# Sums of exponentials over partitions: TensorE's matmuls of a constant in place of GpSimd's reduction

## The chip, the cores and the metric

One Trainium2 chip, one of its cores. The metric is the device time of one execution in microseconds; lower is better.

## The reference

Causal attention with a memory term, then two feed-forward blocks, all in fp32:

```
scores = q @ k^T / sqrt(D), masked above the diagonal       (B, H, S, D = 4, 8, 576, 64)
a      = exp(scores - max);  a /= sum(a) + 1e-9
local  = a @ v
q_p    = phi(q)                                             phi(x) = max(x, exp(x) - 1) + 1 in effect
mem    = (q_p @ M_prev) / (q_p . z_prev + 1e-6)
attn   = g * mem + (1 - g) * local                          g = sigmoid(beta), per head
x      = attn as (2304, 512)
x      = ((x @ w1) * (x @ w2)) @ w3 @ w_out                 d_ff = 1024
h      = x @ w_in;  out = (h * tanh(softplus(h))) @ w_out2  d_ff = 2048
```

What matters here is sum(a): for every head and query, the sum of the exponentials over all keys.

## The kernel before

Heads are worked on in pairs t = 0, 1. A task is a pair of one batch; the four pairs of batch 0 are split into halves of 288 queries, so there are 8 half tasks and 12 whole ones. A task's queries are cut into ranges (one of 288, two of 144, or three of 192), 48 in all, and each range is one step.

Scores lie transposed: keys on the 128 partitions, queries along the free axis, one block for each tile of keys. So the maximum and the sum over keys run over partitions. A step is recorded as these functions:

- SC: score matmuls into a pair of banks ("gp" in the profile), masks, the elementwise maximum over the blocks on VectorE into m ("t"), and then the maximum over partitions on GpSimd (line 556).
- SE: scores minus maximum on VectorE (line 386, "e<-gp,t"), which frees the gp banks, and the exponential on ScalarE. The exponentials E ("e") have four buffers.
- AV, recorded in the step after: E times V. Each pair of heads has 64 output rows per head, done as four matmuls of 32 columns that write the four quarters of one bank ("g<-e,V"), then a copy to mnl on ScalarE.
- SUM, called by AV: adds of E's blocks on VectorE into S (and a copy on ScalarE where the second block is shorter), then partition_all_reduce with add on GpSimd (line 597, "S<-S").
- At a task's last range AV sends the memory term's norm R and row 0 of S through DRAM (d0) into a column layout cp, takes reciprocals there, sends them back broadcast ("Rr"), multiplies mnl by them, adds both terms and splits the result into "x", the input of the feed-forward block. mnl has two buffers.
- MEM: the memory term's matmuls. The first group of a task also holds four matmuls of 32 columns for R, in the same bank behind the outputs.

Between the steps stand fill units: the loading, conversion and products of the first block's weights (fill_w3, fill_w12; "w3" is multiplied with w_out beforehand), and 96 units of the first feed-forward block (ffn1, ffn1o), each 24 matmuls of 288 columns. The main loop gives out units by a credit that grows in each step by RATE, is capped at CMAX, and leaves RES of the ready units untouched. After the last step the remaining units run among the loads of the second block.

Nothing is issued in recorded order. Every operation goes to a recorder with an engine, an estimated cost, its reads and its writes. schedule() then runs a list schedule in estimated time and issues in that order; each engine, and SyncE's one DMA queue, works strictly in that order on the chip. TensorE takes the ready operation recorded first (fill units with a bias GB); other engines take the one with the longest chain behind it, where every operation that feeds TensorE has TensorE's whole remaining chain behind it. An operation of TensorE counts as ready only PEM ns after data from another engine are there. PSUM has four "g" banks and two pairs of "gp" banks.

Of the kernel before, what the change touches and what calls it, by code (L numbers as in the profile page):

```python
# [15 lines left out]
P = 128  # L16
# [4 lines left out]
    AB=10000,  # L21
    GB=200,
    SPLIT=(0,),
    W3P=3,
    W12P=(3, 10),
    RATE=(1.675, 0.949, 2.526, 4.511, 3.527),
    RES=1,
    WARM=40,
    CMAX=3,
    SPM=100,  # L30
    DMM=800,
    PEM=500,
    LA=2,
    F2N=0,
    MIX=10,
# [258 lines left out]
def kernel(  # L294
# [43 lines left out]

    BUFS = {
# [3 lines left out]
        "f": 5, "s": 4, "q": 8, "b": 8, "r": 4, "G": 2, **CFG.get("BUFS", {}),  # L343
    }
# [6 lines left out]
    def buf(tag, shape, dtype=F32):  # L351
        pool = wp if tag[0] == "w" else ROOMS.get(tag, A1)
        return Buf(pool, shape, dtype, tag, BUFS[tag])
# [3 lines left out]
    def gbuf():  # L357
        return Buf(psG, [P, 512], F32, "g", 4)
# [5 lines left out]
    def dma(dst, src, nbytes, r=(), w=()):  # L364
        op("sp", max(500, nbytes / 340.0), lambda: nc.sync.dma_start(out=dst(), in_=src()), r, w)  # L365

    def mm(o, lhsT, rhs, start, stop):
        nc.tensor.matmul(out=o, lhsT=lhsT, rhs=rhs, start=start, stop=stop)  # L368
# [88 lines left out]
    class Task:  # L457


        def __init__(self, g, hfs):  # L460
            self.g, self.hfs = g, hfs
            self.b, self.p = divmod(g, NP)
            self.w = HS * len(hfs)
            self.x0 = HS * hfs[0]
            self.nj = NJ if 1 in hfs else 3
            self.ranges = RANGES[hfs]
            self.e = {}

        def qs(self, q0, q1):
            return slice(q0 - self.x0, q1 - self.x0)  # L470
# [25 lines left out]

    def MEM(T):
        T.mnl = buf("mnl", [P, 2, T.w])
        T.S = buf("S", [P, 2 * T.w])
        T.R = buf("R", [P, T.w // 4])  # L500
        PH, mnl, R, M = T.PH, T.mnl, T.R, T.M
        n = T.w // 4
        for y, hf in enumerate(T.hfs):
            ps = gbuf()
            qs = T.qs(HS * hf, HS * hf + HS)

            def f(ps=ps, qs=qs, y=y):
                for g in range(4):
                    mm(ps.tile[32 * g:32 * g + 32, 0:HS], M.tile[:, 2 + 32 * g:34 + 32 * g], PH.tile[:, qs], True, True)
                if y == 0:  # L510
                    for g in range(4):
                        mm(ps.tile[32 * g:32 * g + 32, HS:HS + n], M.tile[:, 0:32], PH.tile[:, n * g:n * g + n], True, True)

            op("pe", 1.667 * (HS + (n if y == 0 else 0)) + 100, f, r=[PH, M], w=[ps])
            if y == 0:
                act(n, lambda: R.tile, lambda ps=ps: ps.tile[:, HS:HS + n], [ps], [R], True)
            act(HS, lambda qs=qs: mnl.tile[:, 0, qs], lambda ps=ps: ps.tile[:, 0:HS], [ps], [(mnl, (0, hf))], True)

    def SC(T, r):
        qa, qb, tiles = T.ranges[r]  # L520
        n = qb - qa
        d = T.ld
        m = T.m = buf("t", [P, 2 * n])
        T.s = []
        pair = lambda: m.tile.rearrange("p (t n) -> p t n", t=2)
        for i, pieces in enumerate(tiles):
            s = Buf(psA, [P, 2, 512], F32, "gp", 2)
            T.s.append(s)

            def f(s=s, pieces=pieces):  # L530
                for j, q0, q1, c in pieces:
                    kc = (j * P + K3) % SK
                    for t in range(2):
                        mm(s.tile[:, t, c:c + q1 - q0], d.tile[HALF[t], kc:kc + P], d.tile[HALF[t], SK + q0:SK + q1], True, True)

            op("pe", sum(2 * max(0.833 * (q1 - q0), 107) + 10 for _, q0, q1, _ in pieces) + (300 if i == 0 else 0), f, r=T.reads, w=[s])
            part = lambda x, s=s: s.tile[:, :, x[3]:x[3] + x[2] - x[1]]
            mine = lambda x: pair()[:, :, x[1] - qa:x[2] - qa]

            def masks(todo, s=s):  # L540
                for j, q0, q1, c in todo:
                    a, b = max(q0, j * P), min(q1, j * P + P)
                    if a < b:
                        o = lambda c=c + a - q0, w=b - a: s.tile[:, :, c:c + w]
                        op("dve", t_dve(2 * (b - a)), lambda o=o, j=j, a=a, b=b: nc.vector.tensor_tensor(  # L545
                            out=o(), in0=o(), in1=mask[:, a - j * P:b - j * P].unsqueeze(1).to_broadcast([P, 2, b - a]), op=ALU.add), r=[s, fm_], w=[s])

            rest = pieces
            if i == 0:
                masks(pieces[:1])  # L550
                act(2 * n, pair, lambda x=pieces[0], part=part: part(x), [s], [m], True)
                rest = pieces[1:]
            masks(rest)
            for x in rest:
                tt(2 * (x[2] - x[1]), lambda x=x: mine(x), lambda x=x, part=part: part(x), lambda x=x: mine(x), ALU.max, [s, m], [m])
        op("pool", 430 + 2.85 * 2 * n, lambda: nc.gpsimd.partition_all_reduce(m.tile, m.tile, P, bass_isa.ReduceOp.max), r=[m], w=[m])  # L556
# [23 lines left out]
    def SUM(T, r):  # L580

        qa, qb, tiles = T.ranges[r]
        n = qb - qa
        S_, z = T.S, (T.S, r)
        flat = lambda: S_.tile[:, 2 * (qa - T.x0):2 * (qb - T.x0)]
        sv = lambda q0, q1: flat().rearrange("p (t n) -> p t n", t=2)[:, :, q0 - qa:q1 - qa]
        ev = lambda x, q0=None: x[0].tile[:, :, x[1][3] + (q0 - x[1][1] if q0 else 0):x[1][3] + x[1][2] - x[1][1]]
        todo = [(E, x) for E, pieces in T.e[r] for x in pieces]
        first, second = todo[:2]
        q0 = second[1][1]  # L590
        if q0 > qa:
            act(2 * (q0 - qa), lambda: sv(qa, q0), lambda: ev(first)[:, :, 0:q0 - qa], [first[0]], [z])
        tt(2 * (qb - q0), lambda: sv(q0, qb), lambda: ev(first, q0), lambda: ev(second), ALU.add, [first[0], second[0], z], [z])
        for x in todo[2:]:
            a, b = x[1][1:3]
            tt(2 * (b - a), lambda a=a, b=b: sv(a, b), lambda x=x: ev(x), lambda a=a, b=b: sv(a, b), ALU.add, [x[0], z], [z])
        op("pool", 430 + 5.5 * 2 * n, lambda: nc.gpsimd.partition_all_reduce(flat(), flat(), P, bass_isa.ReduceOp.add), r=[z], w=[z])  # L597

    def AV(T, r):
        qa, qb, tiles = T.ranges[r]  # L600
        n = qb - qa
        mnl, W, p = T.mnl, T.w, T.p
        ps = gbuf()
        for x, (E, pieces) in enumerate(T.e[r]):

            def f(E=E, pieces=pieces, x=x):
                for y, (j, q0, q1, c) in enumerate(pieces):
                    for t in range(2):
                        for h in range(2):
                            a = 64 * t + 32 * h  # L610
                            mm(ps.tile[a:a + 32, q0 - qa:q1 - qa], Vf.tile[:, T.i % 2, j, t, 32 * h:32 * h + 32], E.tile[:, t, c:c + q1 - q0],
                               x == y == 0, x == len(tiles) - 1 and y == len(pieces) - 1)

            op("pe", sum(2 * max(0.833 * (q1 - q0), 55) + 30 for _, q0, q1, _ in pieces) + (300 if x == 0 else 0), f, r=[E, (Vf, T.i % 2)], w=[ps])
        act(n, lambda: mnl.tile[:, 1, T.qs(qa, qb)], lambda: ps.tile[:, 0:n], [ps], [(mnl, (1, r))], True)
        SUM(T, r)
        if r < len(T.ranges) - 1:
            return
        ce = W // 32
        R, S_ = T.R, T.S  # L620
        d0 = Buf(dram, [4, W], F32, f"d0_{W}", 2)
        d1 = Buf(dram, [P, ce], F32, f"d1_{W}", 2)
        cp = buf("cp", [P, ce])
        rb = buf("Rr", [P, 2, W])
        for t in range(2):
            dma(lambda t=t: d0.tile[t].rearrange("(g e) -> g e", g=4), lambda t=t: R.tile[t:97 + t:32], 9216, r=[R], w=[(d0, 2 + t)])
        for x, (qa, qb, _) in enumerate(T.ranges):
            dma(lambda a=qa - T.x0, b=qb - T.x0: d0.tile[2:4, a:b].rearrange("(o t) w -> o t w", o=1),
                lambda a=qa - T.x0, b=qb - T.x0: S_.tile[0:1, 2 * a:2 * b].rearrange("o (t w) -> o t w", t=2), 9216, r=[(S_, x)], w=[(d0, (1, x))])
        dma(lambda: cp.tile, lambda: d0.tile.rearrange("r (c e) -> (r c) e", e=ce), 9216, r=[(d0, 2), (d0, 3)] + [(d0, (1, x)) for x in range(len(T.ranges))], w=[cp])  # L630
        cv = lambda: cp.tile
        ts = lambda s, o: lambda: nc.vector.tensor_scalar(out=cv(), in0=cv(), scalar1=s, scalar2=None, op0=o)
        op("dve", 140, ts(eps, ALU.add), r=[cp], w=[cp])
# [420 lines left out]
    for i in range(NS_ + 1):  # L1054
# [33 lines left out]
        def fills(lst):  # L1088
            rec.bias = CFG["GB"]
            for f in lst:  # L1090
                f()
            rec.bias = 0

        fills(mine[0:third])
        SE(T, r)
        fills(mine[third:2 * third])
        if r == 0:
            if T.i + 2 < len(tasks):
# [120 lines left out]
```

## Time and profile before

| | |
|---|---|
| median of 3 runs | 918.91 us (917.59 to 920.21) |
| profiled execution | 921.47 us, its span 919.60 us |
| TensorE busy | 891.5 us (97%) |
| VectorE busy | 735.0 us (80%) |
| ScalarE busy | 445.8 us (48%) |
| GpSimd busy | 196.7 us (21%) |

In the profile's rows PE is TensorE, PEld its weight loads, DVE VectorE, ACT ScalarE, POOL GpSimd, SP SyncE, which issues the transfers. "out<-in" names what is written and read. What stands in brackets is the idle time of the engine just before, and whose work ended it. The last score step lies near 445 us; from then on only the feed-forward blocks run.

### The profile page before, as it was taken

To read this page: it belongs to the slowest core of one execution; us is meant where nothing else is said; L and a number is where in the kernel's file an instruction comes from. 1 tells how busy PE (TensorE), PEld (TensorE's weight loads), DVE (VectorE), ACT (ScalarE), POOL (GpSimd) and SP (SyncE) were. 2 spreads that over 40 slices of the span, in tenths; PEclk is the share of its full clock that TensorE was granted. 3 is DMA by queue.
4 is the path that set the end of the run, shared out by engine and by line. 5 is a ranking of instruction groups with operands and counts; after the bars stand their busy time and mean duration, and the time that the engine had idled before them with its cause. 6 is when DMAs were issued, how large, how long until landed. Compare 5 with 4: busy or idle time off the path is not lost.

```text
span 919.6 us, 20164 instructions
## 1 busy us (share of the span) xinstructions
PE 891.5 (97%) x7992; PEld 809.9 (88%) x7992; DVE 735.0 (80%) x1490; ACT 445.8 (48%) x806; POOL 196.7 (21%) x102
## 2 busy tenths in 40 slices
PE   8899999999999999999999999999999999999998
PEld 6444788777889898898999999999999999999997
DVE  7988999799887678766647598975759999888884
ACT  5569945454444444534335476343426554334431
POOL 3421145655554433444200000000000000000000
PEclk9999999999999999999999999999999999999999
DMA  7668723222323222210169957633325344433441
GB/s 277 219 192 301 252 69 95 92 79 73 96 75 72 72 69 71 59 43 28 27 203 364 370 185 235 214 138 135 130 107 181 144 142 154 137 127 128 131 131 61
DMA packets 60806, 130.49 MB, mean 142 GB/s; under 512 B 11884, under 2 KB 22308, under 8 KB 60712
## 3 DMA queue, kind: packets, MB, share of 16 engines
q1 hardware_dynamic: 60712, 129.20, 42.6%
q8 instruction: 63, 1.03, 0.5%
q14 instruction: 31, 0.25, 0.1%
HBM read 94.80 MB, written 34.37 MB: 140 GB/s over the span
## 4 chain that ended last, share of the span: by engine, by line
PE 59%; DVE 2%; DMA 1%; POOL 0%; issue 0%; ACT 0%; SPq 0%; DVEq 0%; POOLq 0%; ACTq 0%
PE g L368 40%; PE k L368 17%; PE gp L368 1%; DMA Rr<-d 1%; DVE e L386 0%; POOL t L556 0%; DVE S L386 0%; SPq L365 0%; DVE t L386 0%; DVE G L983 0%; DVE mnl L386 0%; DVE u L371 0%; ACT e L378 0%; POOL S L597 0%; DVE gp L545 0%
## 5 line engine op out<-in xcount | busy, mean ns | idle before, releaser
L597 POOL PARTITION_ALL_REDUCE S<-S x48 | 124.1, 2587 | 151.1 <-DVE S L386 106.8
L376 ACT CAST b<-r 128x896 fp32r<-128x896 f32 (+1 forms) x100 | 83.7, 850 | 113.6 <-PE k L368 42.3
L371 DVE TENSOR_TENSOR b<-r,b 128x896 fp32r<-128x896 f32 (+1 forms) x100 | 96.3, 976 | 21.5 <-ACT b L376 21.0
L368 PE MATMUL g<-x,wB 128*128 128x288 f32 x768 | 112.3, 300 | 0.8 <-ACT mnl L376 0.8
L368 PEld LDWEIGHTS g<-x,wB 128*128 128x128 f32 x768 | 104.7, 190 | 5.6 <-issue 2.4
L368 PE MATMUL g<-u,wA 128*128 128x288 f32 x768 | 109.0, 298 | 0.1
L368 PEld LDWEIGHTS g<-u,wA 128*128 128x128 f32 x768 | 103.2, 188 | 5.3 <-issue 2.6
L556 POOL PARTITION_ALL_REDUCE t<-t x48 | 74.2, 1548 | 105.9 <-DVE t L386 94.6
L386 DVE TENSOR_TENSOR e<-gp,t 128x768 f32<-128x768 f32 (+8 forms) x116 | 66.5, 607 | 21.6 <-POOL t L556 21.4
L386 DVE TENSOR_TENSOR r<-r 128x128 f32<-128x128 f32 (+2 forms) x232 | 77.2, 356 | 2.0
L368 PEld LDWEIGHTS gp<-ld 64*128 64x128 f32 x672 | 52.6, 191 | 22.8 <-issue 9.6
L368 PE MATMUL gp<-ld 64*128 64x192 f32 (+6 forms) x672 | 63.3, 321 | 9.3 <-DVE e L386 6.5
L378 ACT ACTIVATE e<-e 128x512 f32<-128x512 f32 (+4 forms) x64 | 54.8, 870 | 29.5 <-DVE e L386 29.2
L368 PE MATMUL g<-wB,wD 128*128 128x512 f32 x128 | 61.6, 625 | 5.8 <-DVE wD L666 3.5
L368 PE MATMUL g<-x,wD 128*128 128x288 f32 x384 | 57.5, 299 | 2.3 <-ACT mnl L376 2.2
L368 PE MATMUL g<-e,V 128*32 128x192 f32 (+6 forms) x1344 | 54.3, 301 | 3.2 <-ACT mnl L376 2.5
L368 PEld LDWEIGHTS g<-x,wD 128*128 128x128 f32 x384 | 52.7, 189 | 5.0 <-ACT mnl L376 2.9
L368 PE MATMUL g<-x,wE 128*128 128x288 f32 x384 | 55.4, 300 | 1.2 <-ACT mnl L376 1.2
L368 PEld LDWEIGHTS g<-x,wE 128*128 128x128 f32 x384 | 51.8, 188 | 4.0 <-ACT mnl L376 1.5
L386 DVE TENSOR_TENSOR t<-gp,t 128x384 f32<-128x384 f32 (+5 forms) x120 | 52.3, 437 | 1.7
L376 ACT CAST u<-t 128x288 fp32r<-128x288 f32 x64 | 27.4, 429 | 53.2 <-DVE t L386 52.9
L368 PEld LDWEIGHTS g<-e,V 128*32 128x32 f32 x1344 | 36.9, 111 | 18.3 <-issue 4.0
(145 smaller groups left out, 1773.5 us busy)
## 6 DMA issues: line engine op xcount, KB each, us to landing
r<-gd SPq DMA_DIRECT2D x72, 256.0 KB
gd<-G SPq DMA_DIRECT2D x32, 512.0 KB
u<-in_moe_w_dram SPq DMA_DIRECT2D x26, 512.0 KB
s<-in_moe_w_out_dram SPq DMA_DIRECT2D x16, 512.0 KB
s<-in_moe_w_in_dram SPq DMA_DIRECT2D x16, 512.0 KB
ld<-in_qk_dram SPq DMA_DIRECT2D x12, 608.0 KB
Rr<-d SPq DMA_DIRECT2D x24, 288.0 KB
kept<-f SPq DMA_DIRECT2D x11, 512.0 KB
```

The lines of the kernel that those rows point to most:

```text
L368: nc.tensor.matmul(out=o, lhsT=lhsT, rhs=rhs, start=start, stop=stop)
L371: eng.tensor_tensor(out=o, in0=a, in1=b, op=ALU.subtract)
L376: op("act", t_act(n, psum), lambda: nc.scalar.copy(out=o(), in_=i()), r, w)
L378: op("act", t_act(n, psum) + more, lambda: nc.scalar.activation(out=o(), in_=i(), func=func, **kw), r, w)
L386: op(eng, t_dve(n) if eng == "dve" else t_pool(n), lambda: e.tensor_tensor(out=o(), in0=a(), in1=b(), op=alu), r, w)
L556: op("pool", 430 + 2.85 * 2 * n, lambda: nc.gpsimd.partition_all_reduce(m.tile, m.tile, P, bass_isa.ReduceOp.max), r=[m], w=[m])
L597: op("pool", 430 + 5.5 * 2 * n, lambda: nc.gpsimd.partition_all_reduce(flat(), flat(), P, bass_isa.ReduceOp.add), r=[z], w=[z])
```

## The change

The reduction on GpSimd is dropped. SUM's adds stay, but SUM is recorded right behind SE, and S has one buffer per range. Behind a range's last AV matmuls stand four matmuls of a constant 128 x 32 of ones, each over a quarter of S, which write the columns n to n + n/2 of the outputs' bank; the last AV operation now reads S too. ScalarE copies these columns into N, ahead of the outputs. A task's sums go from N to DRAM in two transfers, one per head, in place of one per range. Constants of the planner and of the fill are others: fill weights come a step later (W3P, W12P), the rates are mostly lower, RES and CMAX higher, the margin PEM is 700 in place of 500, and the estimated costs of score and AV operations are a little lower.

```diff
-    W3P=3,
-    W12P=(3, 10),
-    RATE=(1.675, 0.949, 2.526, 4.511, 3.527),
-    RES=1,
+    W3P=2,
+    W12P=(4, 10),
+    RATE=(1.575, 1.069, 2.544, 3.632, 3.318),
+    RES=2,
     WARM=40,
-    CMAX=3,
+    CMAX=5,
...
-    PEM=500,
+    PEM=700,
...
     def MEM(T):
-        T.S = buf("S", [P, 2 * T.w])
+        T.N = buf("N", [P, T.w // 2])
...
     def SUM(T, r):
-        S_, z = T.S, (T.S, r)
-        flat = lambda: S_.tile[:, 2 * (qa - T.x0):2 * (qb - T.x0)]
-        sv = lambda q0, q1: flat().rearrange("p (t n) -> p t n", t=2)[:, :, q0 - qa:q1 - qa]
+        z = T.z[r] = buf("S", [P, 2 * n])
+        sv = lambda q0, q1: z.tile.rearrange("p (t n) -> p t n", t=2)[:, :, q0 - qa:q1 - qa]
...
-        op("pool", 430 + 5.5 * 2 * n, lambda: nc.gpsimd.partition_all_reduce(flat(), flat(), P, bass_isa.ReduceOp.add), r=[z], w=[z])
...
     def AV(T, r):
+                if x == len(tiles) - 1:
+                    for g in range(4):
+                        mm(ps.tile[32 * g:32 * g + 32, n:n + n // 2], one.to_broadcast([P, 32]), z.tile[:, n // 2 * g:n // 2 * g + n // 2], True, True)
...
-            op("pe", sum(2 * max(0.833 * (q1 - q0), 55) + 30 for _, q0, q1, _ in pieces) + (300 if x == 0 else 0), f, r=[E, (Vf, T.i % 2)], w=[ps])
+            more = [z] if x == len(tiles) - 1 else []
+            op("pe", sum(2 * max(0.833 * (q1 - q0), 55) + 12 for _, q0, q1, _ in pieces) + (150 if x == 0 else 0) + (0.833 * n + 12 if more else 0), f,
+               r=[E, (Vf, T.i % 2)] + more, w=[ps])
+        c = (qa - T.x0) // 2
+        act(n // 2, lambda c=c: T.N.tile[:, c:c + n // 2], lambda: ps.tile[:, n:n + n // 2], [ps], [(T.N, r)], True)
         act(n, lambda: mnl.tile[:, 1, T.qs(qa, qb)], lambda: ps.tile[:, 0:n], [ps], [(mnl, (1, r))], True)
-        SUM(T, r)
...
-        for x, (qa, qb, _) in enumerate(T.ranges):
-            dma(lambda a=qa - T.x0, b=qb - T.x0: d0.tile[2:4, a:b].rearrange("(o t) w -> o t w", o=1),
-                lambda a=qa - T.x0, b=qb - T.x0: S_.tile[0:1, 2 * a:2 * b].rearrange("o (t w) -> o t w", t=2), 9216, r=[(S_, x)], w=[(d0, (1, x))])
+            dma(lambda t=t: d0.tile[2 + t].rearrange("(r h e) -> h r e", r=k, h=2), lambda t=t: N.tile[64 * t:64 * t + 33:32].rearrange("h (r e) -> h r e", r=k), 9216,
+                r=[(N, x) for x in range(k)], w=[(d0, 4 + t)])
...
         SE(T, r)
+        SUM(T, r)
```

## Rows read from the trace of the kernel before

**Rows 1.** Busy time by engine in four stages; then clock, DMA share, GB/s.
```profile
0.00:100.00 100.00, 89.10 (x524) 50.09 (x525) 84.44 (x177) 70.07 (x130) 28.68 (x17) 0.97 0.76 258
100.00:280.00 180.00, 168.67 (x1956) 145.16 (x1955) 160.26 (x349) 95.84 (x210) 94.83 (x49) 0.97 0.32 92
280.00:452.00 172.00, 170.63 (x1717) 151.76 (x1715) 125.84 (x259) 74.89 (x167) 70.82 (x37) 1.00 0.21 56
452.00:919.60 467.60, 463.12 (x3802) 462.91 (x3800) 364.48 (x706) 205.00 (x301) 2.40 (x1) 1.00 0.49 168
```
**Rows 2.** Timeline of TensorE, the idle times: start, duration, what, idle before and its releaser.
```profile
21.57 1.12 PE L368 MATMUL g<-wB,wD 128*128 128x512 f32 x2 [2.05 <-DVE wB L666]
...
28.68 1.13 PE L368 MATMUL g<-wB,wD 128*128 128x512 f32 x2 [2.64 <-DVE wD L666]
...
48.67 1.02 PE L368 MATMUL g<-e,V 128*32 128x288 f32 x24 [1.47 <-ACT mnl L376]
...
125.17 0.76 PE L368 MATMUL gp<-ld 64*128 64x144 f32 x8 [1.83 <-DVE e L386]
...
195.63 1.85 PE L368 MATMUL g<-x,wB 128*128 128x288 f32 x12 [0.81 <-ACT mnl L376]
...
220.56 2.31 PE L368 MATMUL g<-x,wD 128*128 128x288 f32 x12 [2.18 <-ACT mnl L376]
...
242.19 2.06 PE L368 MATMUL g<-e,V 128*32 128x192 f32 x56 [0.98 <-ACT mnl L376]
...
259.51 3.44 PE L368 MATMUL g<-x,wE 128*128 128x288 f32 x24 [1.24 <-ACT mnl L376]
```
**Rows 3.** Busy times and granted clock in one stretch behind an idle time, columns as above.
```profile
125.70:129.20 3.50, 3.50 (x24) 3.04 (x26) 3.16 (x9) 1.07 (x3) 0.68 (x1) 0.57 0.72 224
```
**Rows 4.** Timelines of GpSimd (the first) and VectorE around the idle times.
```profile
25.56 3.59 POOL L597 PARTITION_ALL_REDUCE S<-S  x1 [3.52 <-DVE S L386]
...
25.71 2.92 DVE L666 SCALAR_TENSOR_TENSOR wD<-wD,u 128x512 int32<-128x512 int32 x1
...
44.44 0.68 DVE L666 SCALAR_TENSOR_TENSOR wD<-wD,u 128x512 int32<-128x512 int32 x1
...
19.38 2.13 DVE L666 SCALAR_TENSOR_TENSOR wB<-wB,wA 128x512 int32<-128x512 int32 x1
...
214.16 2.32 DVE L386 TENSOR_TENSOR mnl<-mnl,Rr 128x1152 f32<-128x1152 f32 x1 [0.25 <-DMA Rr<-d]
...
236.33 1.35 DVE L386 TENSOR_TENSOR mnl<-mnl,Rr 128x1152 f32<-128x1152 f32 x1
...
192.87 2.02 DVE L386 TENSOR_TENSOR mnl<-mnl 128x576 f32<-128x576 f32 x1
...
257.69 0.75 DVE L386 TENSOR_TENSOR mnl<-mnl 128x576 f32<-128x576 f32 x1
...
118.14 1.22 DVE L386 TENSOR_TENSOR S<-e,S 128x288 f32<-128x288 f32 x1
```
**Rows 5.** Groups of instructions: count, then busy us, mean ns, idle before.
```profile
L597 POOL PARTITION_ALL_REDUCE S<-S x48 | 124.1, 2587 | 151.1 <-DVE S L386 106.8 <-issue 28.0 <-ACT S L376 13.8
```
**Rows 6.** Timeline of TensorE, MEM's two groups and what follows each.
```profile
401.28 0.94 PE L368 MATMUL g<-PH,M 128*32 128x288 f32 x16
402.15 1.85 PE L368 MATMUL g<-x,wB 128*128 128x288 f32 x12
403.93 0.69 PE L368 MATMUL g<-PH,M 128*32 128x288 f32 x8
404.55 1.85 PE L368 MATMUL g<-x,wD 128*128 128x288 f32 x12
```
**Rows 7.** Groups of instructions up to 480 us, shapes apart: R's copy.
```profile
L376 ACT COPY R<-g 128x144 f32<-128x144 f32 x12 | 3.4, 282 | 4.4 <-PE g L368 4.4
```
**Rows 8.** Timeline of all engines around one AV: its matmuls and the last add.
```profile
388.71 1.62 PE L368 MATMUL g<-e,V 128*32 128x192 f32 x40
...
390.99 0.55 DVE L386 TENSOR_TENSOR S<-e,S 128x384 f32<-128x384 f32 x1
```

More of the change, by code (lines that the diff above doesn't have):

```diff
@@ L466, in __init__ @@
             self.ranges = RANGES[hfs]
-            self.e = {}
+            self.e, self.z = {}, {}
         def qs(self, q0, q1):
@@ L534, in f @@
                         mm(s.tile[:, t, c:c + q1 - q0], d.tile[HALF[t], kc:kc + P], d.tile[HALF[t], SK + q0:SK + q1], True, True)
-            op("pe", sum(2 * max(0.833 * (q1 - q0), 107) + 10 for _, q0, q1, _ in pieces) + (300 if i == 0 else 0), f, r=T.reads, w=[s])
+            op("pe", sum(2 * max(0.833 * (q1 - q0), 107) + 10 for _, q0, q1, _ in pieces) + (200 if i == 0 else 0), f, r=T.reads, w=[s])
             part = lambda x, s=s: s.tile[:, :, x[3]:x[3] + x[2] - x[1]]
@@ L602, in AV @@
         mnl, W, p = T.mnl, T.w, T.p
-        ps = gbuf()
+        ps, z = gbuf(), T.z[r]
         for x, (E, pieces) in enumerate(T.e[r]):
@@ L619, in AV @@
         ce = W // 32
-        R, S_ = T.R, T.S
+        R, N, k = T.R, T.N, len(T.ranges)
         d0 = Buf(dram, [4, W], F32, f"d0_{W}", 2)
@@ L626, in AV @@
             dma(lambda t=t: d0.tile[t].rearrange("(g e) -> g e", g=4), lambda t=t: R.tile[t:97 + t:32], 9216, r=[R], w=[(d0, 2 + t)])
-        for x, (qa, qb, _) in enumerate(T.ranges):
-            dma(lambda a=qa - T.x0, b=qb - T.x0: d0.tile[2:4, a:b].rearrange("(o t) w -> o t w", o=1),
-                lambda a=qa - T.x0, b=qb - T.x0: S_.tile[0:1, 2 * a:2 * b].rearrange("o (t w) -> o t w", t=2), 9216, r=[(S_, x)], w=[(d0, (1, x))])
-        dma(lambda: cp.tile, lambda: d0.tile.rearrange("r (c e) -> (r c) e", e=ce), 9216, r=[(d0, 2), (d0, 3)] + [(d0, (1, x)) for x in range(len(T.ranges))], w=[cp])
+            dma(lambda t=t: d0.tile[2 + t].rearrange("(r h e) -> h r e", r=k, h=2), lambda t=t: N.tile[64 * t:64 * t + 33:32].rearrange("h (r e) -> h r e", r=k), 9216,
+                r=[(N, x) for x in range(k)], w=[(d0, 4 + t)])
+        dma(lambda: cp.tile, lambda: d0.tile.rearrange("r (c e) -> (r c) e", e=ce), 9216, r=[(d0, x) for x in range(2, 6)], w=[cp])
         cv = lambda: cp.tile
```

2 rows, old and new, of the table BUFS are left out of this document.

## The prediction

> **What bounds the kernel now.** I read the busy times by stage first, then TensorE's timeline for its idle times, then the timelines of VectorE and GpSimd in front of each of them. By stage [rows 1], TensorE is busy for 463 of the last 468 us: after 452 us it is the bound and nothing there is touched. The diff acts on the first 452 us. There TensorE stands idle 10.9 us up to 100, 11.3 us from 100 to 280, and only 1.4 us from 280 to 452. So a microsecond of matmuls added after 280 us costs a microsecond; before, it may fall into a hole. VectorE is the fullest engine beside it, 160 of 180 us in the second stage.
>
> The idle times are few and long [rows 2]: each row gives in brackets how long TensorE stood and whose result ended it. They end on VectorE's wB, wD and e, or on ScalarE's copies to mnl, which themselves wait for a buffer that VectorE's x work frees. Right behind five idle times of 1.79 to 2.64 us lies a stretch of some 3.4 us in which the granted clock is at the lower level, 1.2 in place of 2.4 GHz; one of the five stands in [rows 3] (the window is a little wider, so its mean is 0.57). TensorE is busy in it, so each costs about 3.4/2 = 1.7 us, together 8.5. With the 23.6 us of idle time, 32 us is all that smoother feeding can give.
>
> Why VectorE is late is seen beside GpSimd [rows 4]. At 25.56 GpSimd begins a sum over partitions (3.59 us); VectorE's operation on wD begins at 25.71 and lasts 2.92 us, while the same operation takes 0.68 us at 44.44. It ends at 28.63, and TensorE's idle time ends at 28.68. So too the operation on wB at 19.38 (2.13), the first product on mnl at 214.16 (2.32 against 1.35 at 236.33), the sum on mnl at 192.87 (2.02 against 0.75 at 257.69), an add into S at 118.14 (1.22, against some 0.45 for a tensor operation of that size). VectorE operations that read two tensors in SBUF are held while GpSimd reduces. Those that read PSUM keep their duration.
>
> **What is removed.** The 48 sums on GpSimd, 124.1 us of that engine [rows 5], and with them their holds. I go through the idle times and take what a normal duration would have left:
> - 21.57 and 28.68: 2.13 - 0.68 = 1.45 and 2.92 - 0.68 = 2.24, and the low clock behind the second, 1.7: together 5.4 us.
> - 48.67 (1.47 us, a copy to mnl that waits behind VectorE): sums also lie in front of it, but no hold ends right at it. I count 1.0.
> - 125.17: 1.22 - 0.45 = 0.8 of the 1.83, some 0.3 from small held operations on cp, and the low clock, 1.7: 2.8 us.
> - 195.63: the sum on mnl was held 1.27, the idle time was 0.81, and VectorE's arrears show once more at the next idle time; I count 1.4.
> - 220.56: 2.32 - 1.35 = 1.0 of the 2.18, and the low clock, 1.7: 2.7 us.
> - 242.19: a held sum on mnl again; all 0.98.
> - 259.51: here VectorE waited for the reciprocals' round trip through DRAM. It starts 2.5 us sooner without the GpSimd sum, which is more than the 1.24 us: 1.2.
>
> Together 15.5 us. Two more idle times of the 1.8 to 2.2 us kind, which end at 94 and 173 us, I leave: there ScalarE was full, or the maximum on GpSimd held VectorE, and that stays. Bounds: nothing if other late work stands behind each held operation, 32 us if everything goes.
>
> **What is added on TensorE.** Per range of n queries four matmuls of 32 columns of ones, n/2 moving columns each, side by side in the four quarters of the array. MEM has this very form for R: in [rows 6] the first MEM group (288 and 144 columns) takes 402.15 - 401.28 = 0.87 us, the second (288 alone) 404.55 - 403.93 = 0.62. So four matmuls with 144 columns behind others in the same bank cost 0.25 us, 1.7 ns a column. The 36 ranges with n = 192 have 96 columns (0.163 us), four have 144 (0.245), eight have 72 (0.122): 5.9 + 1.0 + 1.0 = 7.8 us. Upper bound: 288 columns at 1.7 ns are 0.49, so 0.13 us of each group is its start, and if each sum paid that too it were 7.8 + 48 x 0.13 = 14. Lower bound: the 18 ranges after 280 us alone, 2.9, if earlier ones fall into holes. I take 7.8, since the sums follow matmuls of their own shape.
>
> A rule of the Trainium skill speaks for a higher price: the page TensorE: Matmul & The Clock Gate, section Measured speedup vs the span model, lists three column tiles at 2.38 times one, not 3. The price by it would be 7.8 x 3/2.38 = 9.8 us as an estimate and the forecast 2 us later, if the row above did not already hold this loss, being itself a time of four side by side.
>
> **What is added on ScalarE.** 48 copies to N. R's copy of 144 columns takes 282 ns [rows 7]; 48 of at most that are 13.5 us on an engine that is busy 96 of 180 us. The copy stands ahead of the one to mnl, so the bank comes free up to 0.28 us later. TensorE waited some five times for such a copy: 1.4 us at most, 0 at least; I take 1.0.
>
> **What moves.** The adds on VectorE are the same, but are recorded right behind the exponentials, and the last AV matmuls now wait for them. TensorE takes its instructions in order, so behind that wait stand the fill matmuls, and behind AV the bank. In 22 of the 48 ranges the last add now ends after the last AV matmul has started, by 0.08 to 6.97 us, 38.6 us in all; [rows 8] show one, where the add ends at 391.54 and AV's matmuls at 390.33. If the order stayed, that would be the price; at the other end it is nothing. I take 0: the planner sees the new dependence, gives the adds the urgency of TensorE's chain, and keeps AV back by its margin, with fill matmuls in between. The DMA queue loses 48 transfers from S and gains 40 from N, which can start when AV is copied; whatever stands behind them in SyncE's order waits less than for a GpSimd sum. Cost 0.
>
> **The constants.** After batch 0 the rates allow 4 x 2.526 + 4 x 4.511 + 16 x 3.527 = 84.6 fill units before and 77.8 after. Some 7 units of 24 matmuls, 3.5 us each by the twelve of [rows 6], move behind the attention, where TensorE is full: 0, if the fill left over is enough. If 280 to 452 became as leaky as 100 to 280 (6%), it is 172 x 0.063 - 1.4 = 9 us; if the larger margin (PEM) closes the leaks of the second stage it is a gain, already inside the 32. The weights of w3 and w12 are asked for a step later; twelve steps fill the first 100 us and some more, so at worst 8 us, but their loads are of the lowest urgency either way: 0.
>
> **Sum.** -15.5 + 7.8 + 1.0 = -6.7 us. The profiled execution took 921.47 us (span 919.60 and 1.87 around it); it would take 914.8. It lies 2.56 over the median of the runs, 918.91; I predict against the median: 912.
>
> **Rivals.**
> 1. *The adds hold TensorE* (slower). Place: the last AV piece of a range. Price: up to 38.6 us. It decides from 6.7 us on, a sixth of that. For it: VectorE is full in the second stage, and AV now follows what were loose operations. Against: after 280 us VectorE has room, and the planner can order. If a third stays: 912 + 13 = 925.
> 2. *The holes close up again elsewhere* (no change). The maximum on GpSimd goes on holding VectorE, ScalarE and the queue stay late, and half of the 15.5 comes back: 912 + 7.7 = 920.
> 3. *All goes well*: the holes of the first 280 us almost vanish, two thirds of 32 us: 918.9 - 21 + 7.8 = 905, or down to 895 with all of it.
> 4. *The four sums do not run side by side*, though MEM's do, because all read one constant: 4 x 7.8 = 31 us in place of 7.8, 912 + 23 = 935. Only the shared constant speaks for it.
>
> **Chances.** Forecast, 905 to 916: 0.57. Rival 1: 0.14. Rival 2, 916 to 922: 0.14. Rival 3, 895 to 905: 0.12. Rival 4: 0.03. A measurement of this kernel can tell some 0.3% (2.8 us) from no change, so the bounds are 916.2 and 921.7. Faster: 0.57 + 0.12 + 0.04 of rival 2 = 0.73; same: 0.09; slower: 0.14 + 0.03 + 0.01 = 0.18. The range for 8 in 10 is 901 to 922: it leaves some 0.06 below and 0.14 above. The forecast's own is 905 to 916.
>
> **What the profile after would show.** Right: GpSimd busy about 73 us, with the maximum alone; wD, mnl and S operations at their short duration; the sums' matmuls at 0.12 to 0.25 us a range behind AV; TensorE idle less than 15 us before the attention ends; fewer than five stretches at the low clock. Wrong: TensorE waiting for S at the end of AV, idle times of about the old sum with other names in the brackets, or holes after 280 us where the fill has run dry.

## The result and the profile after

The kernel after takes 904.55 us (903.6 to 905.35, 4 runs) against 918.57 for the kernel before: ratio 0.9845, 95% interval 0.9826 to 0.9865, 14.0 us faster. The forecast was 912, 6.6 us under that median. The way was right and the time lies in the range (901 to 922), but the gain is more than twice the forecast; the time is that of rival 3.

Busy times of the kernel after by engine, in the stages of [rows 1], the third one ending with its attention:

```profile
0.00:100.00 100.00, 94.62 (x777) 57.36 (x777) 80.08 (x201) 69.01 (x138) 14.92 (x15) 1.00 0.75 245
100.00:280.00 180.00, 179.09 (x2122) 154.88 (x2120) 158.56 (x360) 111.44 (x256) 35.23 (x23) 1.00 0.36 106
280.00:440.00 160.00, 159.82 (x1730) 143.38 (x1727) 104.46 (x229) 68.54 (x163) 24.38 (x16) 1.00 0.19 53
440.00:901.80 461.80, 457.35 (x3758) 457.14 (x3756) 362.91 (x703) 203.76 (x298) 0.00 (x0) 1.00 0.49 170
```

TensorE's idle time before the end of the attention is 5.4 + 0.9 + 0.2 = 6.5 us, where it was 23.6. The granted clock is 1.00 in all four: none of the five stretches at the lower level is left. The books close on the two spans: 17.1 us of idle time and 5 x 1.7 = 8.5 of low clock are gone. TensorE's other busy time grew by 7.9 (891.5 - 8.5 to 890.9), which is close to the 7.8 foreseen for the sums. Together that is 17.7 of 919.6 - 901.8 = 17.8. (The medians differ by less, since the profiled execution of before lay 2.9 us over its median and that of after 0.9 under.)

What TensorE still waits for, up to 450 us (total us, times, longest), in the kernel after:

```profile
PE g L368 <- DVE wB L669: 2.3, 3, 1.1
PE g L368 <- ACT mnl L376: 1.4, 1, 1.4
PE g L368 <- DVE one L402: 0.9, 1, 0.9
PE gp L368 <- DVE e L386: 0.9, 2, 0.7
PE gp L368 <- issue: 0.8, 1, 0.8
PE g L368 <- ACT N L376: 0.2, 1, 0.2
```

S is not among the names: this profile shows no wait of the last AV matmuls for the adds. Groups of instructions (count, then busy us, mean ns, idle before): the operation on wD in the kernel before, then in the kernel after the reduction that is left and the operation on wD.

```profile
L666 DVE SCALAR_TENSOR_TENSOR wD<-wD,u 128x512 int32<-128x512 int32 x10 | 11.5, 1147 | 2.1 <-ACT wD L378 2.1
...
L556 POOL PARTITION_ALL_REDUCE t<-t x48 | 73.8, 1540 | 348.5 <-DVE t L386 270.5 <-DVE cp L637 21.7 <-DVE cp L635 12.8
L669 DVE SCALAR_TENSOR_TENSOR wD<-wD,u 128x512 int32<-128x512 int32 x10 | 6.9, 688 | 1.2 <-ACT wD L378 1.1
```

The ten operations on wD average 0.69 us after and 1.15 before, where one of them took 2.92 [rows 4]. GpSimd stands idle before the maxima for 349 us in all. A range's sums stand behind AV, ahead of the next fill unit:

```profile
387.16 0.35 PE L368 MATMUL g<-S,one 128*32 128x96 f32 x8
387.44 1.86 PE L368 MATMUL g<-x,wB 128*128 128x288 f32 x12
```

From the sums' start to the fill unit it is 0.28 us. This can still hold the end of AV's own work, so it is no price of the sums; the run with doubled sums, below, gives that.

### The profile page after: what moved, and what is told of

It reads as the page before. It is cut to its first block, busy times and chain, and to the rows that moved or that the text cites. A ratio compares the mean times of both kernels' runs of the same rounds, so it can differ in the third digit from the quotient of the medians.

```text
span 901.8 us, 20879 instructions
## 1 busy us (share of the span) xinstructions
PE 890.9 (99%) x8376; PEld 812.8 (90%) x8376; DVE 706.0 (78%) x1490; ACT 452.8 (50%) x854; POOL 74.5 (8%) x54
## 4 chain that ended last, share of the span: by engine, by line
PE 92%; DVE 4%; DMA 2%; SPq 1%; ACT 1%; issue 1%; DVEq 0%; ACTq 0%
PE g L368 69%; PE k L368 18%; PE gp L368 6%; DVE mnl L386 1%; DMA Rr<-d 1%; DMA wE<-in_moe_w_dram 1%; SPq L365 1%; DVE e L386 1%; DVE S L386 0%; DVE gp L545 0%; DVE t L386 0%; DMA d<-cp 0%; DVE G L986 0%; DVE PH L495 0%; DVE x L371 0%
## 5 line engine op out<-in xcount | busy, mean ns | idle before, releaser
L368 PE MATMUL g<-u,wA 128*128 128x288 f32 x768 | 111.3, 299 | 0.0
L386 DVE TENSOR_TENSOR e<-gp,t 128x768 f32<-128x768 f32 (+8 forms) x116 | 66.3, 606 | 15.6 <-POOL t L556 15.2
L368 PEld LDWEIGHTS gp<-ld 64*128 64x128 f32 x672 | 50.7, 186 | 14.6 <-issue 11.0
L368 PE MATMUL gp<-ld 64*128 64x192 f32 (+6 forms) x672 | 61.4, 315 | 1.7 <-DVE e L386 0.9
L368 PE MATMUL g<-wB,wD 128*128 128x512 f32 x128 | 59.2, 605 | 3.7 <-DVE wB L669 2.3
L942 ACT ACTIVATE G<-G 128x1024 f32<-128x1024 f32 x32 | 33.9, 1060 | 39.7 <-DVE G L386 39.7
L386 DVE TENSOR_TENSOR G<-g,G 128x512 f32<-128x512 f32 (+1 forms) x64 | 39.7, 620 | 16.9 <-PE g L368 14.1
```

Source lines behind the costliest of these rows:

```text
L386: op(eng, t_dve(n) if eng == "dve" else t_pool(n), lambda: e.tensor_tensor(out=o(), in0=a(), in1=b(), op=alu), r, w)
L942: op("act", t_act(1024), lambda: nc.scalar.activation(out=fl(G), in_=fl(G), func=AF.Mish, scale=2.0 ** -8), [G, table], [G])
```

## The experiments

Theory H: GpSimd's sums hold VectorE's operations on two SBUF tensors, as the prediction has it. Theory W: what counted was waiting for GpSimd, either the transfers' wait or that of the maxima which stand behind a sum in GpSimd's queue. Theory C: the constants make the gain. Unless the text says that a run was planned anew, every engine keeps the order of its base kernel. Each ratio below is to runs of the kernel before on the same chip; their medians are 918.4 to 919.0, so a difference between two experiments can be off by some half a microsecond for that reason alone.

**Without the sum.** In the kernel before:

```diff
-        op("pool", 430 + 5.5 * 2 * n, lambda: nc.gpsimd.partition_all_reduce(flat(), flat(), P, bass_isa.ReduceOp.add), r=[z], w=[z])
+        op("pool", 430 + 5.5 * 2 * n, lambda: None, r=[z], w=[z])
```

> The kernel before with every engine's order kept, and GpSimd's sum over partitions left out (row 0 of S holds one partition's sum, so the softmax's denominators are not computed). Theory H, the sums hold VectorE's operations: TensorE's idle time before 452 us falls from 23.4 to about 10 us and the low-clock stretches from five to at most two; time 918.6 - 15 = 903 (899 to 907). Theory W, the gain is the shorter way of the sums to the reciprocals and GpSimd's queue: the same here, so this run only bounds H and W together. Theory C, the new constants make the gain: 916 to 919.

900.46 us, ratio 0.9797 (0.9780 to 0.9813): 18.0 us, inside H's 899 to 907, with TensorE's idle time up to 450 us at 11.2 us (23.6 before) and no low clock there. So the sum on GpSimd cost 18.0 us, not 15.5. C falls as the main cause. The two idle times that the prediction left out, 2.17 and 1.79 us long before, are still there:

```profile
86.30 1.89 PE L368 MATMUL gp<-ld 64*128 64x144 f32 x28 [1.28 <-ACT t L378]
...
161.17 1.09 PE L368 MATMUL gp<-ld 64*128 64x192 f32 x12 [1.73 <-DVE e L386]
```

**A write in the sum's place.** Same place and same waits, but an operation that reads nothing, in the first run seven times over (REP = 7), in the second six times:

```diff
+        op("pool", 430 + 5.5 * 2 * n, lambda: [nc.gpsimd.memset(flat(), 576.0) for _ in range(REP)], r=[z], w=[z])
...
+        op("pool", 430 + 5.5 * 2 * n, lambda: [nc.gpsimd.memset(flat(), 576.0) for _ in range(6)], r=[z], w=[z])
```

> The kernel before with its order and all its waits kept, but in place of each sum over partitions GpSimd writes S seven times over with a constant (the sums are not computed): an operation of about 1.5 to 3 us that reads no tensor, on the same queue, with the same operations waiting for it. Theory H: VectorE's operations keep their short duration, and the time is within 3 us of the run without the sum, near 904. Theory W: the waits are all there, so the time stays near 918, as in the kernel before. In between, the shares of the two.

> The run that writes S seven times took 2.96 us for each in place of the sum's 2.59, and came out at 917.4 although VectorE was no longer held. Here six times, about 2.54 us, so queue and transfers wait as before or a little less and only the hold is gone. If those 0.4 us made the loss: 906 to 912. If the waits for GpSimd make it, whatever their length by a little: 914 to 918.

Seven writes: 917.41 (ratio 0.9988, 0.9977 to 1.0000), H's number missed by 13 us. Six: 907.70 (0.9873, 0.9854 to 0.9891). VectorE is not held in either, as the operation on wD shows, here with six writes (and the write itself; with seven it has 689 ns):

```profile
L597 POOL MEMSET S<- 128x384 f32 x216 | 90.6, 421 | 111.8 <-DVE S L386 83.7 <-ACT S L376 15.1 <-ACT x L376 2.7
...
L666 DVE SCALAR_TENSOR_TENSOR wD<-wD,u 128x512 int32<-128x512 int32 x10 | 6.9, 688 | 1.9 <-ACT wD L378 1.8
```

VectorE's total busy time says the same: 735.0 us before, 705.8 without the sum, 708.3 and 705.8 with six and seven writes. So the sums held VectorE for some 29 us in all.

Taking away the hold alone gains 918.85 - 907.70 = 11 us, at nearly the sum's own length (121.4 us of GpSimd in all against 124.1), and 0.43 us more per range eats almost all of it. What grew is VectorE's wait for a maximum, and TensorE's wait for VectorE's "e"; six writes, then seven:

```profile
DVE e L386 <- POOL t L556: 25.6, 22, 4.1
PE gp L368 <- DVE e L386: 6.4, 11, 1.3
...
DVE e L387 <- POOL t L557: 41.9, 28, 4.6
PE gp L369 <- DVE e L387: 11.3, 13, 2.0
```

A maximum behind a longer operation in GpSimd's queue comes later, the subtraction ("e") with it, and TensorE's next scores wait for the gp banks that the subtraction frees. TensorE's idle time up to 450 us is 16.2 us with six writes and 23.0 with seven; the low clock lasts some 4 and 10 us.

**Transfers freed, the rest kept.** In the kernel before the sum goes to a tile that nothing reads; and then a write of the same place, started by a one-column copy of S so that it waits for the adds:

```diff
+        op("pool", 430 + 5.5 * 2 * n, lambda: nc.gpsimd.partition_all_reduce(spare[:, 0:2 * n], flat(), P, bass_isa.ReduceOp.add), r=[z], w=[z])
...
+        op("pool", 430 + 5.5 * 2 * n, lambda: (nc.gpsimd.tensor_copy(out=spare[:, 0:1], in_=flat()[:, 0:1]), [nc.gpsimd.memset(spare[:, 0:2 * n], 1.0) for _ in range(6)]), r=[z], w=[z])
```

> The kernel before with its order kept and the sum still made on GpSimd, but into a spare tile; the transfers to DRAM take row 0 of S as the adds leave it (so the denominators are one partition's sum), and no longer wait for GpSimd. Left are the hold of VectorE and the maxima's wait in GpSimd's queue. Without any sum it was 900.5, with all 918.4. If hold and queue are the loss: 914 to 919. If the transfers' wait is: 901 to 906.

> The same, but in place of the sum GpSimd copies one column of S (so that it starts when the adds are done) and writes the spare tile six times, some 2.6 us. Left is the maxima's wait in GpSimd's queue alone. If the hold is the loss: 901 to 905. If the queue is: as much as the run with the sum into the spare tile.

The sum into the spare tile: 920.40, ratio 1.0012 (1.0003 to 1.0022). Freeing the transfers gained nothing, so their wait is not the loss. The write: 909.92 (0.9905, 0.9885 to 0.9926), between the two expectations. The difference of these two, 10.5 us, is the hold once more (VectorE busy 736.4 and 707.5 us); and 909.92 lies some 9 us over the run without any sum, which is the queue, with 2.8 us per range in place of the sum's 2.6. So of the 18.0 us the hold is 10.5 to 11 and the queue the other 7 or so. The order of taking them away matters for these figures: no run has the hold without the queue.

**The same in the kernel after.** Behind each range's last add GpSimd also makes the sum, or writes without waiting for the add, or waits and writes:

```diff
+        o = rec.ops[-1]
+        g = o.fn
+        o.fn = lambda: (g(), nc.gpsimd.partition_all_reduce(spare[:, 0:2 * n], z.tile, P, bass_isa.ReduceOp.add))
...
+        o.fn = lambda: (g(), [nc.gpsimd.memset(spare[:, 0:2 * n], 1.0) for _ in range(7)])
...
+        o.fn = lambda: (g(), nc.gpsimd.tensor_copy(out=spare[:, 0:1], in_=z.tile[:, 0:1]), [nc.gpsimd.memset(spare[:, 0:2 * n], 1.0) for _ in range(6)])
```

> The kernel after, with the order of every other engine kept, and GpSimd's sum over partitions given back behind the last add of each range, into a spare tile that nothing reads. TensorE's sums still make the result. Theory H, the reductions hold VectorE: idle time and low clock come back, time 904.6 + 10 to 20 = 915 to 925, with VectorE's operations on two SBUF tensors at 1 to 3 us again. Theory W, waiting for the sum was the cost: no transfer waits for it now, and only the maxima stand behind it in GpSimd's queue, so 905 to 909.

> As the run with the sum beside, but GpSimd writes the spare tile seven times with a constant in place of the sum and reads nothing. The place in GpSimd's queue is like the sum's, but it needs no add, so it may start somewhat sooner. Theory H: VectorE is not held, 904 to 908. If the maxima behind it in the queue make the loss: as much as the run with the sum beside.

> The kernel after with its order kept, and behind each range's adds GpSimd copies one column of S, so that it waits for them, and then writes the spare tile six times. The run that wrote without waiting took 905.4, the one with the sum beside 936.7. If the difference is the hold of VectorE: 904 to 908. If it is that a sum that waits for the adds stands ahead of the maxima in GpSimd's queue: 920 to 937.

936.70 (ratio 1.0192, 1.0175 to 1.0209), 905.42 (0.9854, 0.9839 to 0.9869) and 932.08 (1.0142, 1.0122 to 1.0161). The write that waits for no add fills GpSimd's idle time and costs nothing measurable. A somewhat shorter write (2.8 us a range against 3.0) that starts only after the adds costs 27 us, with VectorE not held (705.8 us busy); the sum, with VectorE busy for 736.3, costs 4.6 more. So H's expectation of 904 to 908 for the last run was wrong by 24 us. Its waits (first TensorE's line, then VectorE's):

```profile
PE gp L368 <- DVE e L386: 19.0, 12, 3.6
DVE e L386 <- POOL t L557: 49.1, 28, 4.4
```

In the kernel after the second is 15.2 us. The queue costs more here than in the kernel before, probably because this plan was made without a sum in it, so that the planner could not put the maxima ahead of it; no run with a new plan shows that.

**The price of the matmuls.**

```diff
-                    for g in range(4):
+                    for g in (0, 1, 2, 3, 0, 1, 2, 3):
```

> The kernel after with the order kept and each range's four sum matmuls issued twice. With the price from the traces, 0.12 to 0.25 us a range: 904.6 + 7.8 = 912 (909 to 913). If they did not run side by side: 904.6 + 31 = 935. If idle time hid them: 905 to 907.

911.59 (ratio 0.9916, 0.9898 to 0.9935), 7.0 us over the kernel after, against 7.8 foreseen, and 31 if they did not run side by side; rival 4 falls.

**The adds at their old place in the record**, planned anew:

```diff
         mnl, W, p = T.mnl, T.w, T.p
+        SUM(T, r)
         ps, z = gbuf(), T.z[r]
...
         SE(T, r)
-        SUM(T, r)
```

> The kernel after with the adds recorded where they were, in the step of AV, right ahead of it, and planned anew. If the earlier place is what keeps TensorE from waiting for the adds: TensorE waits for S at the end of AV, 910 to 925. If the planner orders the adds in time from either place: 903 to 908.

905.82 (ratio 0.9859, 0.9836 to 0.9883), with an interval that overlaps that of the kernel after. TensorE has no wait for S in that profile either. The planner has the adds in time from either place; rival 1 falls.

**The constants.** First the planner's constants of before in the kernel after, and those of after in the kernel before. The expectations count nine; the diff has ten changed numbers in six settings (W3P, W12P, RATE, RES, CMAX, PEM). The estimated costs of score and AV operations are not among them and stay as they are in these two runs.

> The kernel after with the nine constants of the kernel before (the estimated costs stay as after). Theory H: structure makes most of the gain, time 904 to 909. Theory C: 914 to 919, since without the new constants the matmuls' price of 7.8 us eats what is gained.

> The kernel before with the nine constants of the kernel after (the sum stays on GpSimd). Theory H: 915 to 922, as before. Theory C: 905 to 912, since most of the filled idle time came from the larger margin and the later weights.

Then one group at a time undone in the kernel after, in this order: the margin, the pace of the weights, the rates, and the estimated costs. All six runs are planned anew.

```diff
-    PEM=700,
+    PEM=500,
...
-    W3P=2,
-    W12P=(4, 10),
+    W3P=3,
+    W12P=(3, 10),
...
-    RATE=(1.575, 1.069, 2.544, 3.632, 3.318),
-    RES=2,
+    RATE=(1.675, 0.949, 2.526, 4.511, 3.527),
+    RES=1,
...
-    CMAX=5,
+    CMAX=3,
...
-            op("pe", sum(2 * max(0.833 * (q1 - q0), 107) + 10 for _, q0, q1, _ in pieces) + (200 if i == 0 else 0), f, r=T.reads, w=[s])
+            op("pe", sum(2 * max(0.833 * (q1 - q0), 107) + 10 for _, q0, q1, _ in pieces) + (300 if i == 0 else 0), f, r=T.reads, w=[s])
...
-            op("pe", sum(2 * max(0.833 * (q1 - q0), 55) + 12 for _, q0, q1, _ in pieces) + (150 if x == 0 else 0) + (0.833 * n + 12 if more else 0), f,
+            op("pe", sum(2 * max(0.833 * (q1 - q0), 55) + 30 for _, q0, q1, _ in pieces) + (300 if x == 0 else 0) + (0.833 * n + 12 if more else 0), f,
```

> The kernel after with the margin PEM at 500 as before. If the margin makes the 5.3 us: 908 to 911, with more idle time of TensorE from 100 us on. If not: 903 to 906.

> The kernel after with W3P = 3 and W12P = (3, 10) as before, so the weights' units stand a step earlier. With all old constants the kernel after lay 6.8 us at the low clock from 30.9 us on, behind an idle time in the products of the weights. If the pace of the weights makes that: 907 to 911, with the low clock at about 31 us. If not: 903 to 906.

> The kernel after with RATE, RES and CMAX as before: more fill in the attention steps after batch 0, less behind them. If the rates make the 5.3 us: 907 to 911. If TensorE is full either way: 903 to 906.

> The kernel after with the estimated costs of the score and AV matmuls as before (the sums' own estimate stays). The planner then takes these steps for longer by up to 0.3 us. If close estimates matter: 907 to 912. If the order on the engines is what counts and hardly changes: 903 to 907.

| kernel | us | ratio to before (95%) |
|---|---|---|
| after | 904.55 | 0.9845 (0.9826 to 0.9865) |
| after, all old constants | 909.92 | 0.9900 (0.9882 to 0.9919) |
| after, old margin | 906.85 | 0.9870 (0.9847 to 0.9893) |
| after, old pace of the weights | 911.04 | 0.9920 (0.9897 to 0.9942) |
| after, old rates | 910.06 | 0.9905 (0.9883 to 0.9928) |
| after, old estimates | 907.55 | 0.9889 (0.9861 to 0.9917) |
| before, all new constants | 921.35 | 1.0034 (1.0023 to 1.0045) |

In the kernel after the new constants are worth 5.4 us; in the kernel before they cost 2.9. Undone one group at a time, pace and rates each cost as much as all of them together; margin and estimates have intervals that overlap that of the kernel after. So they do not add up, and no single constant carries the 5.4 us. Part of what the old set loses is seen in its trace, in the window of its one stretch at the low clock (columns as in the first fence) and in TensorE's timeline ahead of it:

```profile
30.90:37.70 6.80, 6.17 (x12) 2.06 (x12) 3.59 (x10) 4.83 (x9) 0.00 (x0) 0.50 0.65 198
```

```profile
28.09 1.13 PE L368 MATMUL g<-wB,wD 128*128 128x512 f32 x2 [0.69 <-DVE wB L669]
30.49 1.74 PE L368 MATMUL g<-wB,wD 128*128 128x512 f32 x2 [1.27 <-DVE wB L669]
```

The profiled execution spans 909.2 us, 7.4 more than that of the kernel after, and this stretch is 6.8/2 = 3.4 of them. The pace of the weights alone does not bring it back: that run has its low clock at some 246 us. Holes are not the rest: with all old constants TensorE's idle time up to 450 us is 6.3 us, where the kernel after has 6.5. The rest is nearly all busy time. TensorE is busy for 898.0 us against 890.9 with the same 8376 matmuls, so some 3.7 us beyond the low clock, in small pieces that no run explains. With one group undone there are more holes as well: from 100 to 280 us TensorE is idle for 1.8, 5.1, 3.3 and 4.1 us, in the order of the table, against 0.9 in the kernel after. No run beat the kernel after with the whole computation in it.

## Why the prediction had the direction right and the size short

By the runs the 14.0 us come about so: -18.0 for the sum on GpSimd, +7.0 for the matmuls, some +2.5 for the rest of the edit (900.46 + 7.0 to 909.92, with the old constants), -5.4 for the new ones. Two terms of the sum failed: the constants, put at 0, and what is removed, put at -15.5.

- **What is removed**, -15.5: mis-sized, it is -18.0, and its cause was half told. VectorE's hold, on which the whole term stood, is 10.5 to 11 us. The rest is GpSimd's queue, in which a maximum waits behind a sum. I read the queue only as something that delays the reciprocals, and put idle times that end on "e" down to held operations. That a hold stands right at an idle time showed that it was late, not that it alone was. The two idle times that I left to ScalarE and to the maximum do remain without the sum, at 1.28 and 1.73 us, but the low clock behind them does not, and at 2 x 1.7 = 3.4 us it was left out of the term. That -15.5 comes near to -18.0 with one of two causes is in part luck. The term was also read from one execution with a mean granted clock of 0.990; most other runs of the kernel before have 0.996, so in them the low clock costs less.
- **What is added on TensorE**, +7.8: right, 7.0 measured. MEM's rows gave the price for the same form at other sizes. The Trainium skill's ratio of 2.38 for three column tiles (TensorE: Matmul & The Clock Gate, section Measured speedup vs the span model) gave 9.8 us as an estimate; the measured time lies under that.
- **Copies and bank**, +1.0, and **what moves**, 0: together about +2.5 with the old constants, so small as foreseen; they were not taken apart, and the 2.5 is a balance: the run without the sum has 11.2 us of idle time up to 450 us and no low clock there, the kernel after with the old constants has 6.3 us and one low stretch. TensorE does not wait for S.
- **The constants**, 0: this is the step that failed most; they measured -5.4 (909.92 to 904.55). I looked for a cost of each where TensorE is full, found none, and let the gain from a larger margin count as part of the 32. What the runs show in its place is a gain that hangs on the whole set and on this plan: pace or rates undone alone lose all of it, and the kernel before loses 2.9 us by the set. Of the 7.4 us between the two profiled executions, 3.4 are a stretch at the low clock; nearly all the rest is busy time of TensorE, and why that is shorter with the new constants stays open.
- **The rivals**: 1 and 4 fell to their own runs. 2 did not happen, since taking the sum away gained more than the 15.5. 3 gives the time that was measured, and idle time in the first 280 us did fall from 22.2 to 6.3 us; I gave it 0.12 since I counted only the holes that had a name. It has no term for the constants either, so its time is partly a coincidence.
- **The transfers**, 0: right; freeing them from the sum gained nothing.

Of the signs that were named ahead, these came: GpSimd at 74.5 us, wD at 0.69, idle time under 15 us, no stretch at the low clock. They fit the sum as the cause, but do not say which way it acted.

## What to carry to other kernels

When an engine is taken out of a stage, price two things apart: whom its operations hold while they run, and what stands behind them in its own queue; an operation that reads nothing tells them apart, if its length is the same: here one run with 2.5 us did, and one with 3.0 in place of 2.6 hid the answer. GpSimd at 21% looked idle, but its sums stood ahead of the maxima on which TensorE's next scores hung. And constants of a planner are part of the change: here they gained 0.6% in one kernel and cost 0.3% in the other, so swap them in both before you put them at nothing.

## What was not expected of the hardware

GpSimd's write of 128 x 384 fp32 took 0.42 us, and beside it VectorE's operation on wD kept its 0.69 us in both write runs, where beside a sum it took up to 2.92. The Trainium skill states in SBUF — State Buffer, section Who interferes with whom, that a VectorE instruction with two SBUF inputs contends with a GpSimd instruction that reads SBUF, and not with one that only writes. The traces agree: VectorE is busy for 734.0 to 736.4 us in the four kernels above with a sum on GpSimd, and for 703.2 to 708.9 in all others. The hold goes both ways: in the kernel before, two products on mnl that began before or with a sum, at 236.33 and 191.41 us, kept their 1.35 us, and it was those two sums that took longer, 3.55 and 3.75 us where the median is 2.51. The low clock followed idle times of 0.69 and 1.27 us close together in the kernel after with all old constants, from 30.9 us on, and lasted 6.8 us; the kernel after itself has 0.56, 1.14 and 0.55 us between 27 and 31 us and 1.4 at 43.5, with none behind them.
